# Decoding float64 weights in two VectorE passes instead of three, with an earlier weight schedule and fewer float32 products

## The chip, the core and the metric

The kernel runs on one core of a Trainium2 chip. A core has a matrix engine (TensorE, "PE" in the profile; its weight loads are listed apart as "PEld"), a vector engine (VectorE, "DVE"), an activation engine (ScalarE, "ACT"), a general engine (GpSimd, "POOL") and an engine that here only issues DMAs (SyncE, "SP"). Each engine works through its own list of instructions in the order in which they stand; engines wait for each other by semaphores. The metric is the device time of one execution in microseconds (us), the median of several runs.

## What is computed

Gated causal attention over 8 batches of 8 heads, 576 tokens, 64 values per head, followed by a normalisation and a two-layer feed-forward block with a residual. Cut to what matters:

```python
scores = (q @ k.T) / 8 + cum[:, None] - cum[None, :]     # cum: running sum of log(clip(f))
scores = where(causal, -1e9, scores)
attn   = softmax(scores)
x      = (attn @ v) put back to (8, 576, 512)
xn     = (x - mean(x)) / sqrt(var(x) + 1e-6) * g_ln
out    = x + relu(xn @ w_ch1) @ w_ch2                    # 512 -> 2048 -> 512
```

The two weight matrices arrive as float64; everything else is float32, and the result is float32.

## The kernel before

**Slots.** The 64 heads (`n`) are handled one after the other. A head's 576 query rows are cut into five tiles; tile 0 (64 rows) goes together with tile 1, so a head takes four slots (`t` = 1 to 4) and the attention takes 256 slots (`u`), with three more to drain. In each slot the letters of a string in `ORDERS` say in which order the pieces of work are written out, and this is the order on every engine's list: `Q` products of q and k, `S` mask and row maximum (VectorE), `e` exponential (ScalarE), `B` reciprocal and scaling (VectorE, GpSimd), and for tiles two slots older `t` transposes (TensorE), `h` copies (ScalarE), `l` their low parts (VectorE), then `A` the product with v (TensorE), `F` and `a` its write-out. There are three strings: for slots 0 to 36, 37 to 69, and from 70 on. `P` prepares later heads, with their loads.

**Two forms of products.** A head with `n < NFULL` multiplies with v in float32 (`fac` in `av_unit`; 3 products for the first half of a head and 5 for the second). Every later head splits both factors into a high and a low part of type fp32r and sums products of the parts (`acc` in `av_unit`; 5 and 9 products). The split form needs more around it: `prep_v` splits v (VectorE, GpSimd), `transposed_lo` makes the low parts of the transposed probabilities (VectorE), and the result comes in two halves, which `finish` and `finish_add` put together (ScalarE, VectorE). `NPLAIN = 8` does the same for q and k; it is not touched.

**Weights.** `WPrep` turns the float64 weights into fp32r parts on the chip, in 32 pieces of 128x512 numbers, alternately of layer 1 and layer 2. A float64 is seen as two 32-bit words, high `hw` and low `lw`. `load` brings the words in (512 KB a piece, three buffers `wr`); `scaled` reads the high word as a float32 and multiplies it by 2^-112 on ScalarE, which corrects the exponent (five buffers `wy`); `decode` works on bits, in VectorE passes; for layer 1 `colsum` multiplies with a constant (TensorE, tile `pc`) and `centre` adds the result (four VectorE instructions); `high` and `low` split the piece (ScalarE, GpSimd), and `keep` writes the low part of layer 2 to DRAM, from where it is read as `w2s`. `tick` moves all this on by one piece. How often it runs is set by a line under the letter `W`:

```python
due = 1 + min(u, W_CHANGE) / W_SLOTS + max(0, u - W_CHANGE) * W_TICKS
while not wp.done() and wp.tick_no <= due:
    wp.tick()
```

so a piece is due each `W_SLOTS` slots up to slot 34 and each 1/0.95 slots behind it. The VectorE instructions of a piece are put into `queue` and written out a few at a time by the letters `w` (1), `g` (2) and `f` (3), between the softmax instructions.

**Feed-forward steps.** The second part works on 18 chunks of 256 tokens, each in 16 steps: `mm1` is 12 matmuls with 256 columns (tile `h`), `mm2` 6 matmuls with 512 (tiles `acc`). From slot 35 on a slot takes one step along (letters `M`, `r`, `m`, `N`), where `can` allows it: the step's two weight pieces must be ready, and the chunk's heads done. What is left of the 288 steps behind the last slot runs alone, in the tail.

Of the kernel before, what the change touches and what calls it, by code (L numbers as in the profile page):

```python
# [8 lines left out]
F32 = mybir.dt.float32  # L9
# [3 lines left out]
AF = mybir.ActivationFunctionType  # L13
ALU = mybir.AluOpType
# [10 lines left out]
NEG = -1.0e9  # L25
SCALE = 1.0 / 8.0
NPLAIN = 8
NFULL = 16
W2_LOW = 3
W2_WAIT = 2  # L30
ALL = 2 * NCHUNK * FT + W2_WAIT
# [1 line left out]
FIRST_MOE = 35  # L33
WARM = 36

W_SLOTS, W_CHANGE, W_TICKS = 2.4, 34, 0.95
W_RAW, W_FLOAT = 3, 5
W_BORROW = 2
W_SUMS = 2
# [19 lines left out]
def attn_moe(ctx: ExitStack, tc: tile.TileContext, qk, v, f, g, w1, w2, out):  # L59
    nc = tc.nc  # L60
# [14 lines left out]
    def m2(name, dt):  # L75
        return work.tile([P, 512], dt, tag="m2", bufs=11, name=name)
# [9 lines left out]
    for i in range(WARM):  # L86
# [4 lines left out]
        out=mask[:, S - P :], in_=mask[:, S - P :], pattern=[[-1, P]], base=0,  # L91
# [42 lines left out]
    class WPrep:  # L134
# [21 lines left out]
        def scaled(self, n):  # L156
            layer, j = self.items[n]
            d = self.d[n]
            if layer == 1 and self.tick_no < W_BORROW:
                d["y"] = m2(f"wy{layer}_{j}", U32)  # L160
            else:
                d["y"] = wpool.tile([P, DM], U32, tag="wy", bufs=W_FLOAT, name=f"wy{layer}_{j}")
            nc.scalar.activation(d["y"].bitcast(F32), d["hw"].bitcast(F32), AF.Copy, scale=2.0**-112)

        def decode(self, n):
            layer, j = self.items[n]
            d = self.d[n]
            y, z, low = d["y"], d["hw"], d["lw"]
            d["w"] = y.bitcast(F32)
            ve = nc.vector  # L170

            return [
                lambda: ve.tensor_scalar(out=z, in0=z, scalar1=0x80000000, scalar2=None, op0=ALU.bitwise_and),
                lambda: ve.scalar_tensor_tensor(  # L174
                    out=y, in0=y, scalar=3, in1=z, op0=ALU.logical_shift_left, op1=ALU.bitwise_or
                ),
                lambda: ve.scalar_tensor_tensor(
                    out=y, in0=low, scalar=29, in1=y, op0=ALU.logical_shift_right, op1=ALU.bitwise_or
                ),
            ]  # L180

# [123 lines left out]
    def load(n):  # L305
        h = Head()
        h.n, h.plain, h.full = n, n < NPLAIN, n < NFULL
        if h.plain:
# [356 lines left out]
    class Moe:  # L665
# [21 lines left out]
        low = []  # L687
# [211 lines left out]
```

## Time and profile before

| | |
|---|---|
| median of 3 runs | 1253.7 us (1252.57, 1253.70, 1260.37) |
| profiled execution, first to last instruction | 1260.6 us |
| PE busy | 1230.2 us, 98% of the span |
| DVE busy | 782.8 us, 62% |
| ACT busy | 645.2 us, 51% |
| POOL busy | 426.8 us, 34% |
| DMA | 190.77 MB, mean 151 GB/s |
| chain that ended last | PE 86%, DVE 5%, DMA 4% |

The profile lists only the span of the profiled execution. It is as long as the slowest of the three timed runs, so there is next to nothing around it. A busy PE in this profile is not a PE at its peak, since the ends of matmuls are modelled; idle time of the PE is what its row lacks to the length of a stretch.

### The profile page before, as it was taken

The page shows a single profiled execution, that of the slowest core. Times are in us where ns is not written, and L with a number is a line of the kernel's source. Part 1 is how long each engine was busy: PE and PEld are TensorE (multiplying, and loading weights), DVE is VectorE, ACT ScalarE, POOL GpSimd, SP SyncE. Part 2 cuts the span into 40 slices and gives each one's busy share as a digit, 9 for nine tenths or more (in the row PEclk, how much of TensorE's full clock was granted, in tenths as well). Part 3 has the DMA queues.
Part 4 walks back from the last instruction along what each step waited for, and adds up shares of the span by engine and source line. Part 5 has one row for each costly group of instructions (what it writes and reads, how often), then busy time and mean ns, then how long its engine had stood idle before and what let it go on. Part 6 is the DMA issues. An engine that isn't in the chain of part 4 may idle for free.

```text
span 1260.6 us, 25515 instructions
## 1 busy us (share of the span) xinstructions
PE 1230.2 (98%) x8148; PEld 1085.2 (86%) x8148; DVE 782.8 (62%) x2868; ACT 645.2 (51%) x1920; POOL 426.8 (34%) x529
## 2 busy tenths in 40 slices
PE   8997898999999999999999999999999999999998
PEld 5554686889999999999999999999999999999997
DVE  5587888357576768576767666666767673233232
ACT  5577666555555556565656555655555552112111
POOL 3356556333343334334443434343434330000000
PEclk7799899999999999999999999999999999999999
DMA  5366674544554545444545454545454534444432
GB/s 154 110 183 204 198 240 160 159 124 155 154 165 148 168 141 171 137 150 149 156 144 160 145 168 151 168 151 166 149 152 147 168 104 136 125 126 117 151 109 92
DMA packets 139381, 190.77 MB, mean 151 GB/s; under 512 B 32496, under 2 KB 81648, under 8 KB 139248
## 3 DMA queue, kind: packets, MB, share of 16 engines
q1 hardware_dynamic: 139248, 189.15, 49.0%
q8 instruction: 65, 1.06, 0.3%
q14 instruction: 68, 0.56, 0.1%
HBM read 157.46 MB, written 23.36 MB: 143 GB/s over the span
## 4 chain that ended last, share of the span: by engine, by line
PE 86%; DVE 5%; DMA 4%; ACT 1%; POOL 1%; issue 1%; SPq 0%; DVEq 0%; POOLq 0%; ACTq 0%
PE h L580 11%; PE h L581 10%; PE h L582 10%; PE acc L602 10%; PE acc L603 10%; PE acc L604 10%; PE tr L418 7%; PE o L503 5%; PE o L481 3%; PE s L370 3%; PE s L371 3%; DMA raw<-in_qk_dram 3%; PE s L368 1%; PE xp L418 1%; DVE wy L174 1%
## 5 line engine op out<-in xcount | busy, mean ns | idle before, releaser
L412 POOL TENSOR_SCALAR p<-p,st 64x64 f32<-64x64 f32 (+4 forms) x320 | 173.8, 546 | 568.1 <-DVE st L411 225.9
L580 PE MATMUL h<-x,w1h 128*128 128x256 f32 x1152 | 329.6, 286 | 0.0
L581 PE MATMUL h<-x,w1h 128*128 128x256 f32 x1152 | 325.9, 283 | 0.7 <-DVE x L565 0.7
L582 PE MATMUL h<-x,w1l 128*128 128x256 f32 x1152 | 324.9, 282 | 0.0
L588 ACT ACTIVATE hh<-h 128x256 fp32r<-128x256 f32 x288 | 110.4, 383 | 287.7 <-PE h L582 281.0
L593 DVE SCALAR_TENSOR_TENSOR hh<-h,hh 128x256 fp32r<-128x256 f32 x288 | 121.4, 422 | 193.3 <-ACT hh L588 189.0
L602 PE MATMUL acc<-w2h,hh 128*128 128x512 f32 x576 | 228.1, 396 | 0.0
L603 PE MATMUL acc<-w2s,hh 128*128 128x512 f32 x576 | 226.4, 393 | 0.0
L604 PE MATMUL acc<-w2h,hh 128*128 128x512 f32 x576 | 225.7, 392 | 0.0
L580 PEld LDWEIGHTS h<-x,w1h 128*128 128x128 f32 x1152 | 218.2, 189 | 5.2 <-issue 0.9
L581 PEld LDWEIGHTS h<-x,w1h 128*128 128x128 f32 x1152 | 218.2, 189 | 4.6 <-DVE x L565 1.3
L582 PEld LDWEIGHTS h<-x,w1l 128*128 128x128 f32 x1152 | 218.0, 189 | 0.0
L405 ACT ACTIVATE p<-p,st 64x64 f32<-64x64 f32 (+4 forms) x320 | 178.3, 558 | 60.8 <-DVE st L394 58.1
L468 ACT CAST ph<-tr 64x128 fp32r<-64x128 f32 (+4 forms) x384 | 108.6, 332 | 110.4 <-PE tr L418 82.6
L418 PE MATMUL tr<-identr,p 128*128 128x128 f32 (+1 forms) x896 | 143.7, 277 | 9.0 <-POOL p L412 4.7
L394 DVE CUSTOM_DVE_ANT_0 p<-s,mask 64x64 f32<-64x64 f32 (+4 forms) x320 | 130.3, 420 | 15.5 <-PE s L368 9.8
L418 PEld LDWEIGHTS tr<-identr,p 128*128 128x128 f32 (+1 forms) x896 | 102.9, 132 | 35.3 <-POOL p L412 9.1
L604 PEld LDWEIGHTS acc<-w2h,hh 128*128 128x128 f32 x576 | 108.2, 188 | 25.3
L473 DVE TENSOR_TENSOR ph<-tr,ph 64x192 fp32r<-64x192 f32 x192 | 57.8, 301 | 106.1 <-ACT ph L468 102.9
L602 PEld LDWEIGHTS acc<-w2h,hh 128*128 128x128 f32 x576 | 108.7, 189 | 13.4 <-issue 0.9
L603 PEld LDWEIGHTS acc<-w2s,hh 128*128 128x128 f32 x576 | 109.0, 189 | 12.3
L370 PE MATMUL s<-hi 128*64 128x64 f32 x336 | 109.8, 349 | 8.3 <-POOL hi L348 6.5
(81 smaller groups left out, 1848.4 us busy)
## 6 DMA issues: line engine op xcount, KB each, us to landing
w2s<-w2d SPq DMA_DIRECT2D x288, 256.0 KB
raw<-in_qk_dram SPq DMA_DIRECT2D x56, 576.0 KB
wr<-in_w_dram SPq DMA_DIRECT2D x32, 512.0 KB
vr<-in_v_dram SPq DMA_DIRECT2D x64, 160.0 KB
out_dram<-xt SPq DMA_DIRECT2D x36, 256.0 KB
xq<-hi SPq DMA_DIRECT2D x56, 144.0 KB
xa<-xs SPq DMA_DIRECT2D x32, 160.0 KB
w2d<-wl SPq DMA_DIRECT2D x16, 256.0 KB
```

What stands on the lines that cost most here:

```text
L370: mm(sp, h.hi[:, 0, q0 : q0 + m], h.hi[:, 1, a:z], start=True, stop=False)
L394: nc.vector.tensor_tensor_reduce(out=pt[:m, a:z], in0=sp, in1=mask[:m, off + a : off + z], scale=-SCALE, scalar=3.0e38 if i == 0 else st[: ...
L405: nc.scalar.activation(pt[:m, :w], pt[:m, :w], AF.Exp, bias=st[:m, i : i + 1], scale=-1.0, accum_out=st[:m, 2:3])
L412: nc.gpsimd.tensor_scalar(out=pt[:m, :w], in0=pt[:m, :w], scalar1=st[:m, 3:4], scalar2=1.0, op0=ALU.mult, op1=ALU.mult)
L418: nc.tensor.transpose(out_, in_, ident[:m, :m])
L580: mm(ph, w1h[:, k, fs], c.x[k][:, 0, :], start=(k == 0), stop=False)
L581: mm(ph, w1h[:, k, fs], c.x[k][:, 1, :], start=False, stop=False)
L582: mm(ph, w1l[:, k, fs], c.x[k][:, 0, :], start=False, stop=(k == KT - 1))
L593: nc.vector.scalar_tensor_tensor(out=h[:, 1, :], in0=ph, scalar=0.0, in1=h[:, 0, :].bitcast(F32), op0=ALU.max, op1=ALU.subtract)
L602: mm(c.acc[i], h[:, 0, ts_], w2h[:, j, :], start=(j == 0), stop=False)
L603: mm(c.acc[i], h[:, 0, ts_], low, start=False, stop=False)
L604: mm(c.acc[i], h[:, 1, ts_], w2h[:, j, :], start=False, stop=(j == FT - 1))
```

## The change

`NFULL` goes from 16 to 12: heads 12 to 15 take the split form of the product with v. `W_SLOTS` goes from 2.4 to 1.6: up to slot 34 a weight piece is due each 1.6 slots. `scaled` uses a Relu with a slope for negative numbers in place of a scaled copy: positive numbers are multiplied by 2^-112, negative ones by 2^-112 times 2^32. The extra 32 in the exponent field of a negative number becomes its sign bit when the word is shifted left by 3, so the pass that kept the sign falls away: `decode` has a shift of the low word and one shift-and-or, no longer three passes.

```diff
-NFULL = 16
+NFULL = 12
...
-W_SLOTS, W_CHANGE, W_TICKS = 2.4, 34, 0.95
+W_SLOTS, W_CHANGE, W_TICKS = 1.6, 34, 0.95
...
-            nc.scalar.activation(d["y"].bitcast(F32), d["hw"].bitcast(F32), AF.Copy, scale=2.0**-112)
+            nc.scalar.activation(d["y"].bitcast(F32), d["hw"].bitcast(F32), AF.Prelu, scale=2.0**-112, alpha=2.0**32)
...
-                lambda: ve.tensor_scalar(out=z, in0=z, scalar1=0x80000000, scalar2=None, op0=ALU.bitwise_and),
+                lambda: ve.tensor_scalar(out=low, in0=low, scalar1=29, scalar2=None, op0=ALU.logical_shift_right),
                 lambda: ve.scalar_tensor_tensor(
-                    out=y, in0=y, scalar=3, in1=z, op0=ALU.logical_shift_left, op1=ALU.bitwise_or
-                ),
-                lambda: ve.scalar_tensor_tensor(
-                    out=y, in0=low, scalar=29, in1=y, op0=ALU.logical_shift_right, op1=ALU.bitwise_or
+                    out=y, in0=y, scalar=3, in1=low, op0=ALU.logical_shift_left, op1=ALU.bitwise_or
                 ),
```

Three lines fall away, so everything behind `decode` stands three lines higher in the changed kernel (L580 becomes L577).

What this does to the lists of the engines is seen in three places. The first is VectorE in slots 12 and 13 (head 3, tiles 1 and 2). `L394`/`L391` is mask and maximum, `L410`/`L407` and `L411`/`L408` are sum and reciprocal, `L173`, `L174` and `L177` are the passes of `decode`, `L194` is `centre`. Before:

```order
L394 ISA p_1_543,st_1_544<-s_1_0_534,mask 128x192
L394 ISA st_1_544 128x1
L174 SCALAR_TENSOR_TENSOR wy_3_505<-wy_3_505,wr_3_400 128x512
L177 SCALAR_TENSOR_TENSOR wy_3_505<-wr_3_400,wy_3_505 128x512
L410 TENSOR_SCALAR st_0_541<-st_0_541 64x1
L411 RECIPROCAL st_0_541<-st_0_541 64x1
L410 TENSOR_SCALAR st_1_544<-st_1_544 128x1
L411 RECIPROCAL st_1_544<-st_1_544 128x1
L394 ISA p_2_578,st_2_579<-s_2_0_576,mask 128x320
```

And in the changed kernel:

```order
L391 ISA p_1_564,st_1_565<-s_1_0_555,mask 128x192
L391 ISA st_1_565 128x1
L174 SCALAR_TENSOR_TENSOR wy_4_527<-wy_4_527,wr_4_423 128x512
L407 TENSOR_SCALAR st_0_562<-st_0_562 64x1
L408 RECIPROCAL st_0_562<-st_0_562 64x1
L407 TENSOR_SCALAR st_1_565<-st_1_565 128x1
L408 RECIPROCAL st_1_565<-st_1_565 128x1
L173 TENSOR_SCALAR wr_4_490<-wr_4_490 128x512
L391 ISA p_2_607,st_2_608<-s_2_0_605,mask 128x320
L391 ISA st_2_608 128x1
L194 SCALAR_TENSOR_TENSOR wy_3_420<-wy_3_420,gcol,pc_557 128x128
L174 SCALAR_TENSOR_TENSOR wy_4_582<-wy_4_582,wr_4_490 128x512
```

One large pass instead of two stands between maximum and reciprocal; but the next piece follows at once, and slot 13, which had no weight work, now has a large pass and the first part of a centring.

The second place is VectorE in slot 46 (head 11, tile 3), where `L593`/`L590` is a feed-forward step's `mm1_low` and `L565`/`L562` is `chunk_split`. Before:

```order
L394 ISA p_3_1929,st_3_1930<-s_3_0_1926,mask 128x448
L394 ISA st_3_1930 128x1
L174 SCALAR_TENSOR_TENSOR wy_13_1910<-wy_13_1910,wr_13_1784 128x512
L177 SCALAR_TENSOR_TENSOR wy_13_1910<-wr_13_1784,wy_13_1910 128x512
L593 SCALAR_TENSOR_TENSOR hh_8_1978<-h_8_1948,hh_8_1978 128x256
L410 TENSOR_SCALAR st_3_1930<-st_3_1930 128x1
L411 RECIPROCAL st_3_1930<-st_3_1930 128x1
L565 TENSOR_TENSOR x_0_1991<-xr_0_1916,x_0_1991 128x256
L173 TENSOR_SCALAR wr_13_1859<-wr_13_1859 128x512
```

In the changed kernel:

```order
L391 ISA p_3_1987,st_3_1988<-s_3_0_1984,mask 128x448
L391 ISA st_3_1988 128x1
L194 SCALAR_TENSOR_TENSOR wy_15_1785<-wy_15_1785,gcol,pc_1931 128x128 x3
L590 SCALAR_TENSOR_TENSOR hh_8_2031<-h_8_2001,hh_8_2031 128x256
L407 TENSOR_SCALAR st_3_1988<-st_3_1988 128x1
L408 RECIPROCAL st_3_1988<-st_3_1988 128x1
L562 TENSOR_TENSOR x_0_2043<-xr_0_1974,x_0_2043 128x256
```

The last weight piece is centred here, and no weight work stands on VectorE from slot 47 on; before, it went on to slot 53.

The third place is TensorE in slot 52 (head 13, tile 1; the product with v is that of head 12). `L481` is the float32 product, `L500` the split one, `L189` is `colsum`, `L602` and `L603` belong to `mm2`, `L577` to `L579` are `mm1`. Before:

```order
L189 MATMUL pc_2307<-wy_15_2171,gneg 128x128 x4
L418 MATMUL tr_3_2313<-identr,p_3_2202 64x128
L418 MATMUL tr_3_2313<-identr,p_3_2202 128x128 x3
L481 MATMUL o_2_2318<-ph_12_2210,vr_1965 64x320
L481 MATMUL o_2_2318<-ph_12_2210,vr_1965 64x256
L481 MATMUL o_2_2318<-ph_12_2210,vr_1965 64x128
L602 MATMUL acc_0_1498<-w2h,hh_11_2284 128x512
L603 MATMUL acc_0_1498<-w2s_2243,hh_11_2284 128x512
```

In the changed kernel:

```order
L415 MATMUL tr_3_2370<-identr,p_3_2237 64x128
L415 MATMUL tr_3_2370<-identr,p_3_2237 128x128 x3
L500 MATMUL o_2_2375<-ph_12_2240,vv_2269 128x320
L500 MATMUL o_2_2375<-ph_12_2240,vv_2269 128x256
L500 MATMUL o_2_2375<-ph_12_2240,vv_2269 128x128
L500 MATMUL o_2_2375<-pl_12_2241,vv_2269 64x256
L500 MATMUL o_2_2375<-pl_12_2241,vv_2269 64x128
L577 MATMUL h_14_2381<-x_0_1436,w1h 128x256
L578 MATMUL h_14_2381<-x_0_1436,w1h 128x256
L579 MATMUL h_14_2381<-x_0_1436,w1l 128x256
```

Before, slots 48, 50, 52, 54 and 56 have no `mm1`, because the weights aren't there yet; in the changed kernel each of them has one, and slot 70 lacks one instead (its chunk's heads aren't there). Both lists start with `mm1` in slot 38. Behind slot 255 there are 76 steps left before and 72 now.

More of the change, by code (lines that the diff above doesn't have):

```diff
@@ L167, in decode @@
             d = self.d[n]
-            y, z, low = d["y"], d["hw"], d["lw"]
+            y, low = d["y"], d["lw"]
             d["w"] = y.bitcast(F32)
```

## The prediction

> **What bounds the kernel now.** I read the stages first, since the whole-span shares mix stages with different limits. In this view, busy time by stretch, the columns are length, busy us and instructions (x) of each engine, granted TensorE clock, DMA share and GB/s.
>
> ```profile
> core 0: us, PE busy (x) PEld busy (x) DVE busy (x) ACT busy (x) POOL busy (x), PEclk, DMA share, GB/s
> 11.00:52.00 41.00, 39.31 (x133) 24.34 (x131) 22.84 (x86) 20.74 (x65) 11.80 (x18) 0.63 0.47 130
> 52.00:96.00 44.00, 40.77 (x198) 24.82 (x196) 33.67 (x124) 31.34 (x99) 22.07 (x27) 0.96 0.55 161
> 96.00:137.00 41.00, 28.12 (x138) 18.25 (x138) 30.30 (x91) 26.55 (x79) 26.95 (x28) 0.88 0.62 191
> 137.00:185.00 48.00, 48.00 (x317) 40.70 (x316) 43.98 (x116) 30.93 (x84) 27.19 (x26) 1.00 0.72 227
> 185.00:225.00 40.00, 35.71 (x221) 27.89 (x220) 29.90 (x102) 26.68 (x79) 23.11 (x25) 1.00 0.52 169
> 400.00:900.00 500.00, 499.76 (x3532) 460.34 (x3532) 347.95 (x1359) 289.68 (x877) 193.19 (x245) 1.00 0.51 156
> 1040.00:1240.00 200.00, 200.00 (x1297) 182.20 (x1297) 58.04 (x173) 37.72 (x99) 0.00 (x0) 1.00 0.43 128
> ```
>
> From 225 us on TensorE never waits, so there only its own work counts. Before that it idles 12.9 us in 96 to 137 and 4.3 us in 185 to 225. In 137 to 185 TensorE is full and VectorE nearly so (92%). In 11 to 52 TensorE is full at 0.63 of its clock. The stretches are, by slot: 0 to 27 up to 96 us, 28 to 37 up to 137, 38 to 47 up to 185, 48 to 57 up to 225.
>
> The same view for the tile `h` alone counts feed-forward steps: 12 matmuls, one VectorE and one ScalarE instruction each.
>
> ```profile
> core 0: us, PE busy (x) PEld busy (x) DVE busy (x) ACT busy (x), PEclk, DMA share, GB/s
> 185.00:225.00 40.00, 8.39 (x60) 7.48 (x60) 2.09 (x5) 1.83 (x5) 1.00 0.52 169
> 400.00:900.00 500.00, 196.44 (x1467) 187.39 (x1466) 51.75 (x123) 47.31 (x123) 1.00 0.51 156
> 1040.00:1240.00 200.00, 110.98 (x832) 107.63 (x831) 29.61 (x70) 26.88 (x70) 1.00 0.43 128
> ```
>
> In the tail a step takes 200/70 = 2.86 us of TensorE. A slot with a step takes 500/123 = 4.07 us, so the attention part of a slot with split products is 1.21 us. In 185 to 225 there are only 5 steps in ten slots: the weights come too late for more.
>
> **The change part by part.** The chain that ended last, in order of time, shows a head's product with v in both forms, on a TensorE that waits for nothing:
>
> ```profile
> 252.69 1.47 PE o L481 x6
> 261.57 2.23 PE o L481 x10
> 271.28 0.50 PE o L503 x5
> 278.74 0.94 PE o L503 x9
> ```
>
> *Four heads in split form.* In float32 the two halves of a head take 1.47 + 2.23 = 3.70 us, in split form 0.50 + 0.94 = 1.44. Heads 12 to 15 do this from slot 51 to 66, where TensorE sets the time: 4 x 2.26 = **-9.0 us**. What the split form adds lies on other engines. By form:
>
> ```profile
> L473 DVE TENSOR_TENSOR pl<-tr,ph 128x384 fp32r<-128x384 f32 x96 | 53.6, 558 | 2.2
> L473 DVE TENSOR_TENSOR ph<-tr,ph 64x128 fp32r<-64x128 f32 x144 | 40.9, 284 | 65.9 <-ACT ph L468 63.7 <-ACT ot L537 0.3
> L354 DVE CAST vv<-vr 128x320 fp32r<-128x320 f32 x48 | 23.1, 481 | 1.8 <-PE o L481 1.8
> L548 DVE TENSOR_TENSOR xs<-o,ot 64x320 f32<-64x320 f32 x48 | 23.1, 481 | 0.7
> ```
>
> These and their smaller forms come to some 4.7 us of VectorE a head, 1.2 a slot. The stretch 400 to 900 already holds them and has VectorE at 348 of 500 us, 2.8 of each slot's 4.07; so TensorE hides them, provided that no weight work is left there. None is: VectorE's list ends it in slot 46. If 2.2 us of weight work a slot still lay there, VectorE would need 5.0 us and the gain would be gone.
>
> *Steps that come earlier.* Slots 48, 50, 52, 54 and 56 get their step, and TensorE has the time for it: its idle 4.3 us in 185 to 225. Where it loses them is seen in the timeline:
>
> ```profile
> 188.32 0.67 ACT L337 CAST hi<-raw 128x576 fp32r<-128x576 f32 x1 [2.56 <-DMA raw<-in_qk_dram]
> 192.75 0.47 PE L370 MATMUL s<-hi 128*128 128x448 f32 x1 [1.83 <-DVE st L394]
> ```
>
> VectorE with its weight queue (and a head's load, which stays) is late, and TensorE has no step to fill the gap. With a step in every slot it has. I take **-4.3 us**, all of it; the ends are 0 and -6 (a busy TensorE is not quite a full one, since the ends of matmuls are modelled). The five steps come out of the tail; slot 70 lacks one, which costs nothing if TensorE stays fed in it, and at most a step, 2.9 us: **+1**.
>
> *`colsum` moves ahead.* Its rows by stretch:
>
> ```profile
> 11.00:52.00 41.00, 4.99 (x24) 4.86 (x24) 0.63 0.47 130
> 185.00:225.00 40.00, 2.13 (x16) 2.02 (x16) 1.00 0.52 169
> ```
>
> The 16 records in the full stretch go (-2.1 us). One piece more, 8 records at 0.21 us, falls into 11 to 52, where TensorE is full too (+1.7): **-0.4** together.
>
> *Two passes.* These are the groups of weight work:
>
> ```profile
> L174 DVE SCALAR_TENSOR_TENSOR wy<-wy,wr 128x512 uint32<-128x512 uint32 x32 | 35.3, 1103 | 0.0
> L177 DVE SCALAR_TENSOR_TENSOR wy<-wr,wy 128x512 uint32<-128x512 uint32 x32 | 30.2, 945 | 0.6
> L173 DVE TENSOR_SCALAR wr<-wr 128x512 uint32<-128x512 uint32 x32 | 16.9, 528 | 0.8 <-ACT wy L163 0.8
> L197 DVE SCALAR_TENSOR_TENSOR wy<-wy,gcol,pc 128x128 f32<-128x128 f32 x64 | 20.7, 337 | 0.0
> L163 ACT ACTIVATE wy<-wr 128x512 f32<-128x512 f32 x32 | 21.5, 671 | 8.3 <-POOL w1l L218 3.6 <-DMA wr<-in_w_dram 2.7 <-POOL wl L218 1.9
> L214 ACT CAST w1h<-wy 128x512 fp32r<-128x512 f32 x16 | 9.9, 617 | 17.3 <-DVE wy L197 17.2
> L218 POOL TENSOR_TENSOR w1l<-wy,w1h 128x512 fp32r<-128x512 f32 x16 | 22.7, 1416 | 0.1
> ```
>
> A piece costs VectorE 0.53 + 1.10 + 0.94 + 0.67 (half of four times 0.337) = 3.25 us now, and 2.30 without L177. The shift takes L173's place with the same tile, so I take 0.53 for it (at best nothing, at worst L174's 1.10). The Relu with a slope isn't in the trace; I take the scaled copy's 0.67 us, the nearest row; the ends are L214's 0.62 for as many elements and two full passes, 1.34.
>
> For the SBUF page of the Trainium skill (SBUF — State Buffer, section "SBUF: two separate sides") a VectorE instruction with two inputs and a GpSimd one exclude each other for a whole instruction. The trace agrees: the medians by tile are 1.06 us for L174 and 0.69 for L177, with equal minima. By that rule the wait falls on whichever two-input pass comes first behind GpSimd, and the dropped one is the cheap one: a piece gets 0.69 us cheaper, not 0.94. That would take 1 us off the next term.
>
> *96 to 137 us.* From slot 34 on a piece is due each 1.05 slots in both kernels, so VectorE gets 0.9 us a slot lighter. What stood there:
>
> ```profile
> 107.48 4.56 DMA raw<-in_qk_dram
> 121.38 4.93 DMA raw<-in_qk_dram
> ...
> 131.91 0.82 PE L418 MATMUL tr<-identr,p 128*64 128x128 f32 x3 [4.12 <-DVE wy L197]
> 132.66 4.20 PE L481 MATMUL o<-ph,vr 64*64 64x256 f32 x10
> ```
>
> The two loads of `raw` are in the chain and stay: there is one such buffer, and the next load waits for the last reader. The 4.12 us of idle TensorE are a PSUM bank that late `centre` work holds, and the product behind it takes 4.20 us instead of 2.23, at half the clock. Four slots at 0.9 us are 3.8 of VectorE's; I take **-4 us**. The bounds are 0 (the loads set the pace anyway) and -9 (the stall, the slow product and some more of the 12.9 idle us).
>
> *Slots 0 to 33.* Pieces each 1.6 slots mean 0.21 more of them a slot: VectorE 0.625 x 2.30 = 1.44 us instead of 0.417 x 3.25 = 1.36, ScalarE +0.27 (L163 and L214), GpSimd +0.29 (L218). No engine is near its limit by that (in 52 to 96 VectorE has 34 of 44 us, ScalarE 31, GpSimd 22), but softmax instructions queue behind this work on each. The order helps: between maximum and reciprocal, where VectorE waits for the exponential anyway, L174 alone stands now instead of L174 and L177. I take **+1 us**; the ends are -3 (0.1 us a slot better) and +9 (all of ScalarE's 0.27 us in 34 slots). The piece loads have room: L163 waited 2.7 us for them in all, and DMA is at 0.55.
>
> 137 to 185 stays at its floor, TensorE. The sum is -9.0 - 4.3 + 1 - 0.4 - 4 + 1 = -15.7 us on the profiled execution's 1260.6, which is as long as the slowest run (1260.37), 6.9 above the median. I carry the same difference to the median: 1253.7 - 15.7 = **1238 us**.
>
> **The rivals.**
>
> *Early slots pay.* The chain in 96 to 137 runs through the `raw` loads, so a lighter VectorE brings nothing there, and ScalarE's added work delays every exponential: -9.0 - 4.3 + 1 - 0.4 + 0 + 9 = -3.7, **1250 us**. For it speaks that the loads are in the chain; against it that the late `centre` stalled TensorE for 4 us.
>
> *Everything early loosens.* The stall and both slow products in 96 to 137 go (-9), slots 0 to 33 gain 3 us, and slot 70 costs nothing: -9.0 - 4.3 - 0.4 - 9 - 3 = -25.7, **1228 us**.
>
> *The clock stays low: slower than before.* Exponentials counted by stretch, with the granted clock in the column behind them:
>
> ```profile
> 14.00:44.00 30.00, 6.33 (x20) 0.50 0.41 108
> 61.40:96.00 34.60, 10.37 (x32) 1.00 0.63 185
> ```
>
> A head has ten such records, so a slot took 3.75 us at half the clock and 2.70 at full. It came back at 44 us; more ScalarE and GpSimd work ahead of the transposes could open gaps on TensorE that keep it low up to slot 37: 26 slots x 1.05 = +27, the gain in 96 to 137 is lost, and -9.0 - 4.3 + 1 - 0.4 + 1 + 27 = +15.3 gives **1269 us**. From some 11 such slots on (11.7 / 1.05) the kernel is slower than before. Against it: in 52 to 96 the clock was 0.96 though TensorE had gaps. The Trainium skill (TensorE: Matmul & The Clock Gate, Part 1) says that a window of some 3.4 us without enough activity halves the clock; the row above agrees with the two rates, and the 4.12 us gap at 128 is the kind that it means.
>
> *It doesn't do what it says.* VectorE, not TensorE, sets slots 48 to 66, because weight work hangs over from slot 46: the -9.0 and -4.3 shrink to some -6 together (less than half), and 1253.7 - 6 + 1 - 0.4 - 4 + 1 = **1245 us**.
>
> **How the numbers follow.** Forecast (1231 to 1244) 0.53, everything loosens 0.17, early slots pay 0.18, hang-over 0.07, low clock 0.05. A measurement tells 1% from no change, here 1241.2 and 1266.2. Faster by over 1% are the looser case and nearly all of the forecast, 0.68; within 1% the early and the hang-over case and the forecast's upper end, 0.27; slower the low clock, 0.05. The range reaches from below the looser case (a Relu or shift at their good ends adds little) to the early case's end: 1222 to 1251.
>
> **What would show it.** A step in each slot from 38 to 69 and no idle TensorE in 185 to 225; L500 at 0.50 and 0.94 us in heads 12 to 15; 72 steps behind the last slot; L163 at 0.67 us and L173 at 0.53; slot 28 reached near 96 us and slot 48 near 182; no 4 us stall behind `centre`. Wrong would make it: a slower L163, slots 0 to 33 longer by more than 3 us, half the clock behind 60 us, or VectorE over 4 us a slot in slots 48 to 51.

## The result and the profile after

The changed kernel takes **1240.1 us** (median of 4 runs, 1238.05 to 1240.83), the kernel before 1253.1 us beside it (4 runs, 1250.88 to 1260.37): a ratio of 0.9869, 95% interval [0.983, 0.9909]. That is 13.0 us less; 1238 had been forecast, from 15.7 us less. The ratios given here and below are not the quotients of the two medians; that would be 0.9896 here.

The two profiled executions differ by more, 21.6 us:

```profile
span 1239.0 us, 25554 instructions
...
PE 1215.1 (98%) x8140; PEld 1080.7 (87%) x8140; DVE 767.6 (62%) x2884; ACT 647.6 (52%) x1920; POOL 427.3 (34%) x533
...
PEclk8997999999999999999999999999999999999999
...
PE 89%; DVE 3%; ACT 2%; DMA 2%; POOL 1%; issue 1%; SPq 0%; DVEq 0%; POOLq 0%; ACTq 0%
```

The profiled execution of before was one of its long ones (1260.6 us of span), that of after an ordinary one (1239.0 us of span in a run of 1240.83, 0.7 us over the median). So the stretches of before and after must not be subtracted without asking which difference another execution would show again. The busy time by stretch of the changed kernel:

```profile
core 0: us, PE busy (x) PEld busy (x) DVE busy (x) ACT busy (x) POOL busy (x), PEclk, DMA share, GB/s
11.00:52.00 41.00, 36.67 (x168) 22.44 (x166) 29.81 (x114) 28.92 (x88) 17.97 (x26) 0.88 0.72 204
96.00:137.00 41.00, 35.69 (x182) 25.60 (x181) 29.39 (x94) 27.99 (x78) 27.48 (x27) 0.83 0.71 220
137.00:185.00 48.00, 48.00 (x305) 39.78 (x304) 24.32 (x88) 28.97 (x85) 26.68 (x27) 1.00 0.56 172
185.00:225.00 40.00, 40.00 (x280) 36.56 (x279) 28.41 (x111) 21.03 (x64) 14.50 (x19) 1.00 0.45 142
217.00:282.00 65.00, 60.81 (x417) 55.29 (x416) 41.96 (x164) 32.79 (x100) 23.81 (x29) 0.97 0.47 146
400.00:900.00 500.00, 499.75 (x3531) 460.36 (x3531) 347.86 (x1348) 288.05 (x874) 195.93 (x246) 1.00 0.50 155
```

Three things are to be seen. TensorE has no idle time left in 185 to 225, where it had 4.3 us (these are slots 50 to 59 here and 48 to 57 before; slots 48 to 57, 173.64 to 217.44 us here, are full as well, 43.80 of 43.80 us). VectorE has 24.32 us of work in 137 to 185 in place of 43.98, and TensorE stays full there. And there is a new hole: in 217 to 282 TensorE lacks 4.2 us, at a clock of 0.97, where the prediction let it wait for nothing.

The same view for the tile `h` alone shows ten feed-forward steps in 185 to 225 in place of five (slots 48 to 57 hold ten too):

```profile
185.00:225.00 40.00, 16.65 (x120) 14.92 (x120) 4.22 (x10) 3.75 (x10) 1.00 0.45 142
```

The weight work by groups (line, engine, operation, busy us and mean ns, idle time before with what ended it):

```profile
L163 ACT ACTIVATE wy<-wr 128x512 f32<-128x512 f32 x32 | 21.4, 670 | 10.8 <-POOL wl L215 5.1 <-DMA wr<-in_w_dram 3.2 <-POOL w1l L215 2.4
L173 DVE TENSOR_SCALAR wr<-wr 128x512 uint32<-128x512 uint32 x32 | 17.4, 544 | 0.0
L174 DVE SCALAR_TENSOR_TENSOR wy<-wy,wr 128x512 uint32<-128x512 uint32 x32 | 34.9, 1091 | 0.1
L211 ACT CAST w1h<-wy 128x512 fp32r<-128x512 f32 x16 | 9.8, 615 | 3.3 <-DVE wy L194 3.3
L415 PE MATMUL tr<-identr,p 128*64 128x128 f32 x320 | 77.4, 273 | 5.5 <-ACT xs L531 2.3 <-POOL p L409 2.2 <-DVE st L391 0.9
```

The Relu with a slope costs what the scaled copy cost, 0.670 us, and the shift 0.544. ScalarE's `high` waits 3.3 us for `centre` in all, where it waited 17.2, and in the row of the transposes, the last, a PSUM bank held by `centre` ends no wait any more.

**The new wait** stands at the start of slot 64. SyncE's own queue first, then ScalarE, VectorE, TensorE and GpSimd in the timeline (start, length, instruction; in brackets the idle time ahead of it and what ended it):

```profile
237.00 0.43 SPq L610 DMA_DIRECT2D xw<-xa  x1
...
240.33 1.33 SPq L610 DMA_DIRECT2D xw<-xb  x1
241.76 0.38 SPq L692 DMA_DIRECT2D w2s<-w2d  x1
242.18 0.44 SPq L316 DMA_DIRECT2D raw<-in_qk_dram  x1
```

```profile
246.53 0.67 ACT L334 CAST hi<-raw 128x576 fp32r<-128x576 f32 x1 [3.84 <-DMA raw<-in_qk_dram]
...
248.87 0.42 DVE L590 SCALAR_TENSOR_TENSOR hh<-h,hh 128x256 fp32r<-128x256 f32 x1 [5.29 <-ACT hh L585]
...
249.34 0.38 PE L577 MATMUL h<-x,w1h 128*128 128x256 f32 x1 [2.73 <-DVE st L407]
...
249.70 0.71 POOL L409 TENSOR_SCALAR p<-p,st 64x64 f32<-64x64 f32 x2 [7.81 <-DVE st L407]
```

Eight small loads (`rows_load` of chunk 1, whose steps now come five earlier) occupy SyncE's queue from 237.00 to 241.66, and the load of a head's `raw` is issued behind them. ScalarE stands at `hi<-raw` for 3.84 us; behind it in its list are the exponentials and the feed-forward's Relu, so VectorE, GpSimd and in the end TensorE stand too. The chain that ended last goes this way: the load of `raw` takes 4.26 us from its issue, then ScalarE, VectorE and TensorE follow. Before, chunk 1 ran five steps later, and its loads did not stand ahead of this `raw`.

### The profile page after: what moved, and what is told of

It is laid out like the page before. It is cut to its first block, busy times and chain, and to the rows that moved or that the text cites. A ratio compares the mean times of both kernels' runs of the same rounds, so it can differ in the third digit from the quotient of the medians.

```text
span 1239.0 us, 25554 instructions
## 1 busy us (share of the span) xinstructions
PE 1215.1 (98%) x8140; PEld 1080.7 (87%) x8140; DVE 767.6 (62%) x2884; ACT 647.6 (52%) x1920; POOL 427.3 (34%) x533
## 4 chain that ended last, share of the span: by engine, by line
PE 89%; DVE 3%; ACT 2%; DMA 2%; POOL 1%; issue 1%; SPq 0%; DVEq 0%; POOLq 0%; ACTq 0%
PE h L577 11%; PE h L578 11%; PE h L579 11%; PE acc L599 11%; PE acc L600 10%; PE acc L601 10%; PE tr L415 7%; PE o L500 6%; PE s L367 3%; PE s L368 3%; PE o L478 2%; PE xp L415 1%; DMA raw<-in_qk_dram 1%; PE s L365 1%; PE pc L186 1%
## 5 line engine op out<-in xcount | busy, mean ns | idle before, releaser
L577 PE MATMUL h<-x,w1h 128*128 128x256 f32 x1152 | 330.1, 287 | 3.5 <-DVE st L407 2.7
L579 PE MATMUL h<-x,w1l 128*128 128x256 f32 x1152 | 325.2, 282 | 0.0
L590 DVE SCALAR_TENSOR_TENSOR hh<-h,hh 128x256 fp32r<-128x256 f32 x288 | 121.5, 422 | 187.0 <-ACT hh L585 174.2
L577 PEld LDWEIGHTS h<-x,w1h 128*128 128x128 f32 x1152 | 218.4, 190 | 8.5 <-DVE st L407 3.0
L579 PEld LDWEIGHTS h<-x,w1l 128*128 128x128 f32 x1152 | 218.3, 189 | 0.0
L465 ACT CAST ph<-tr 64x128 fp32r<-64x128 f32 (+4 forms) x416 | 117.9, 332 | 131.1 <-PE tr L415 100.8
L415 PE MATMUL tr<-identr,p 128*128 128x128 f32 (+1 forms) x896 | 141.2, 274 | 5.5 <-ACT xs L531 2.3
L391 DVE CUSTOM_DVE_ANT_0 p<-s,mask 64x64 f32<-64x64 f32 (+4 forms) x320 | 130.2, 419 | 7.7 <-PE s L368 2.8
L470 DVE TENSOR_TENSOR ph<-tr,ph 64x192 fp32r<-64x192 f32 x208 | 62.6, 301 | 114.5 <-ACT ph L465 111.6
```

What stands on the lines that cost most here:

```text
L391: nc.vector.tensor_tensor_reduce(out=pt[:m, a:z], in0=sp, in1=mask[:m, off + a : off + z], scale=-SCALE, scalar=3.0e38 if i == 0 else st[: ...
L415: nc.tensor.transpose(out_, in_, ident[:m, :m])
L577: mm(ph, w1h[:, k, fs], c.x[k][:, 0, :], start=(k == 0), stop=False)
L579: mm(ph, w1l[:, k, fs], c.x[k][:, 0, :], start=False, stop=(k == KT - 1))
L590: nc.vector.scalar_tensor_tensor(out=h[:, 1, :], in0=ph, scalar=0.0, in1=h[:, 0, :].bitcast(F32), op0=ALU.max, op1=ALU.subtract)
```

## The experiments

Each kernel ran beside runs of the kernel before on its chip; the ratio is to these. They took 1255.8 us (median of 27) beside the first four experiments and 1256.9 us (median of 11) beside the four from the changed kernel again to ten float32 heads. Because executions of one kernel differ early and agree late, I read every profile in two parts: up to the start of slot 48 (VectorE's first mask instruction of that slot), and from there to the end. In all of these kernels ten steps lie ahead of slot 48.

```
                                  slot 28   slot 34   slot 48      end    slot 48 to end
before                               95.9     115.1     184.9   1260.6        1075.8
heads alone                          84.0     105.5     175.0   1247.4        1072.3
two passes alone                     86.2     108.5     175.8   1248.3        1072.4
two passes and early slots           88.8     107.9     171.4   1242.5        1071.0
heads and early slots, three passes 101.6     121.5     189.1   1253.5        1064.4
changed                              88.2     108.2     173.6   1239.0        1065.4
changed, again                       89.0     108.2     175.6   1241.0        1065.4
rows loaded earlier                  90.6     110.0     175.4   1234.9        1059.5
  and a piece each 1.4 slots         92.8     114.7     180.1   1239.8        1059.7
  and ten float32 heads              92.6     115.1     179.4   1240.6        1061.2
```

The last column repeats to 0.1 us in the two profiles of the changed kernel, and in five profiles of the kernel in the last line it was 1059.2 to 1061.6. The first columns can move much further: see the second experiment.

### The parts one by one

**Two passes alone.** Against the changed kernel:

```diff
-NFULL = 12
+NFULL = 16
-W_SLOTS, W_CHANGE, W_TICKS = 1.6, 34, 0.95
+W_SLOTS, W_CHANGE, W_TICKS = 2.4, 34, 0.95
```

> The kernel before with the two-pass decoding alone (a piece each 2.4 slots, 16 float32 heads). Theory A (the TensorE account of the prediction: the gain is the four heads and the steps that come earlier, and slots 0 to 33 gain nothing): the weights still come too late for steps in slots 48 to 57, only stalls behind a late VectorE go, some 2 us in 96 to 137 and some 2 in 185 to 225, so 1249 us, ratio 0.997. Theory B (the two passes shorten the early softmax chain and keep TensorE's clock up, as the profile after suggests, where slot 28 is reached 7.6 us earlier): most of that stays, 1244 us or less, ratio 0.992 or less.

Measured: 1250.1 us (10 runs), ratio 0.9952 [0.9927, 0.9976], so theory A's size. From slot 48 on the kernel is 3.4 us shorter (1075.8 to 1072.4) though it still misses the five steps. TensorE's idle time in slots 48 to 57 (175.85 to 213.60 us here) goes all the same, with VectorE lighter there (33.24 us of work in 50, where the kernel before has 29.90 in 40):

```profile
175.00:225.00 50.00, 49.22 (x310) 38.95 (x309) 33.24 (x121) 32.92 (x98) 27.98 (x30) 1.00 0.62 197
```

**Heads alone.** Against the kernel before:

```diff
-NFULL = 16
+NFULL = 12
```

> The kernel before with float32 products in 12 heads, three passes and a piece each 2.4 slots. Theory A: weight work stays on VectorE up to slot 53, beside the split heads' 1.2 us a slot, so slots 48 to 53 are bound by VectorE at 5 us or more and a good part of the 9.0 us is lost: 1249 us, ratio 0.996. Rival (TensorE sets these slots anyway): the full 9 us, 1244 us, ratio 0.993.

Measured: 1250.4 us (12 runs), ratio 0.9963 [0.9936, 0.9989]. Of the 9.0 us for four heads only 3.5 show from slot 48 on. VectorE still has weight work there and now splits heads as well: it has 41.92 us of work in 50, and TensorE lacks 7.9 us. Of the waits that the profile lists for TensorE in 174 to 226, 7.3 us end on VectorE and 0.4 on GpSimd:

```profile
175.00:225.00 50.00, 42.08 (x267) 35.16 (x266) 41.92 (x143) 29.91 (x88) 28.97 (x31) 0.97 0.49 157
```

This is the hang-over rival's mechanism, seen where the schedule was not moved. The same profile tells something else. VectorE's list is that of the kernel before, in the same order, up to slot 48, and yet it reaches slot 28 at 84.0 us and not at 95.9, and slot 48 at 175.0 and not at 184.9:

```profile
11.00:52.00 41.00, 36.82 (x175) 22.78 (x175) 30.30 (x115) 27.87 (x89) 17.62 (x26) 0.92 0.58 159
```

The clock granted in 11 to 52 was 0.92 here and 0.63 in the profile of before. So the earlier marks of the changed kernel (slot 28 at 88.2) are no gain by themselves.

**Two passes and early slots,** without the heads. Against the changed kernel:

```diff
-NFULL = 12
+NFULL = 16
```

> The changed kernel with 16 float32 heads again. Theory A: the heads 12 to 15 cost TensorE 9.0 us more than in the changed kernel, and nothing hides them: 1249 us, ratio 0.996 to before. Rival (the split heads' extra VectorE and ScalarE work takes their gain back, so the heads bring nothing): 1240 us, ratio 0.990.

Measured: 1244.2 us (6 runs), ratio 0.9914 [0.9891, 0.9938], between the two theories and nearer to the rival; theory A's 0.996 lies outside the interval. From slot 48 on it is 4.8 us shorter than before, and the changed kernel is 5.6 us shorter still, so the heads do bring something and the rival's reason is wrong. What brings this kernel so low lies ahead of slot 48 (see the account of the prediction). The same eight loads stand ahead of `raw` here, but ScalarE waits 1.79 us, and TensorE, with float32 products still to do, hardly lacks anything:

```profile
218.00:285.00 67.00, 66.56 (x430) 56.08 (x429) 32.97 (x140) 32.55 (x100) 22.22 (x28) 1.00 0.44 137
```

**Heads and early slots with three passes.** Against the kernel before:

```diff
-NFULL = 16
+NFULL = 12
-W_SLOTS, W_CHANGE, W_TICKS = 2.4, 34, 0.95
+W_SLOTS, W_CHANGE, W_TICKS = 1.6, 34, 0.95
```

> The changed kernel with the three-pass decoding again: a piece each 1.6 slots and 12 float32 heads stay. Theory A: a piece costs VectorE 3.25 us, 2.0 a slot up to slot 33 instead of 1.4, and between maximum and reciprocal two large passes stand again; slots 0 to 33 get 0.2 to 0.5 us longer each, and slots 34 to 44 are full on VectorE: 1250 to 1258 us, ratio 0.998 to 1.004. Rival (the earlier schedule and the heads do it alone, the dropped pass was hidden): 1240 us, ratio 0.990.

Measured: 1250.9 us (12 runs), ratio 0.9962 [0.9945, 0.9979], close to theory A. This is the kernel that shows what the passes are for. From slot 48 on it is as fast as the changed kernel (1064.4 and 1065.4), so heads and schedule bring the whole of the late gain without them. But it is slower in all: 4.9 us under the kernel before beside it, where the changed kernel is 13.0 and 15.3 us under it in its two sets of runs. That lies ahead of slot 48, which its profile reaches at 189.1 us and the changed kernel's at 173.6. The profiled run was its longest, 4.4 us over its median; some 11 us are left. VectorE's share grows in the early stretch:

```profile
11.00:52.00 41.00, 36.65 (x159) 22.43 (x157) 32.91 (x115) 27.63 (x83) 18.93 (x26) 0.83 0.70 190
```

With three passes, a piece each 1.6 slots costs early what it brings late; the ratio is the one of heads alone.

### The new wait

**The changed kernel again,** as the base of the next three on one chip.

> The changed kernel itself, timed beside the next three on the same chip: 1240 us, ratio 0.987.

Measured: 1241.6 us (6 runs), ratio 0.9863 [0.9826, 0.9899]; ScalarE's wait for `raw` at slot 64 was 4.04 us this time.

**Rows loaded earlier.** The first half of chunk 1's rows is loaded one step earlier, so that the eight loads no longer stand just ahead of `raw`:

```diff
-                if c.j in (FT - 7, FT - 5):
-                    rows_load(c, (c.j - (FT - 7)) // 2)
+                first = FT - 8 if c.n == 1 else FT - 7
+                if c.j in (first, FT - 5):
+                    rows_load(c, 0 if c.j == first else 1)
```

> The changed kernel with the first row loads of chunk 1 issued one step earlier, so that eight small loads no longer stand ahead of a raw load on SP's queue at slot 63. Theory A (what the four heads lost was this new wait: ScalarE waits 3.84 us for raw at slot 64, TensorE 2.73 us, and then runs 3.4 us at half the clock): 3 to 4 us less than the changed kernel, 1236 to 1237 us, ratio 0.984, and no idle TensorE near slot 64. Rival (the raw load waits for its buffer anyway and takes its 4 to 5 us, whatever is ahead of it): within 1 us of the changed kernel, ratio 0.987.

Measured: **1235.8 us** (6 runs, 1234.68 to 1236.83), ratio 0.9817 [0.9778, 0.9856]: 5.8 us below the changed kernel beside it, whose fastest run took 1238.47. Counted from the start of slot 48, the load of `raw` is issued 64.4 us on, where it was 68.5 in the first profile of the changed kernel. ScalarE's wait is 0.24 us, and the stretch is full:

```profile
244.68 0.68 ACT L334 CAST hi<-raw 128x576 fp32r<-128x576 f32 x1 [0.24 <-DMA xw<-xb]
```

```profile
241.00:256.00 15.00, 15.00 (x108) 13.71 (x106) 9.27 (x35) 8.74 (x26) 6.03 (x8) 1.00 0.44 148
217.00:282.00 65.00, 63.90 (x447) 58.30 (x447) 44.90 (x174) 35.94 (x111) 25.39 (x31) 1.00 0.50 157
```

In the changed kernel the stretch 241 to 256 had 12.27 us of TensorE at a clock of 0.89. The late part falls from 1065.4 to 1059.5, 5.9 us, so all of the gain lies from slot 48 on. It is more than the 2.7 us of idle time and more than the 3 to 4 us of theory A. The hole also cost clock: the trace of the changed kernel has half the clock for some 3.4 us, 249.9 to 253.3, so 1.7 us of work at full clock. These two make 4.4 us, near the 4.6 by which slots 48 to 67 get shorter (91.2 to 86.6). The other 1.3 us come behind slot 67, in a part that takes 972.9 to 974.7 us in the kernels with early slots; their cause is not shown. This is the fastest version that ran.

**A piece each 1.4 early slots,** on top of that:

```diff
-W_SLOTS, W_CHANGE, W_TICKS = 1.6, 34, 0.95
+W_SLOTS, W_CHANGE, W_TICKS = 1.4, 34, 0.95
```

> The last kernel with a piece each 1.4 slots in slots 0 to 33. Theory A: 0.09 pieces more a slot bring VectorE 0.2 us a slot there, and slots 0 to 33 aren't bound by it: within 2 us of the last kernel, 1235 to 1239 us. Rival (early slots pay for each piece, some 2 us of in-order work each): three more pieces by slot 34, 4 to 6 us slower, 1241 us or more.

Measured: 1242.0 us (6 runs), ratio 0.9868 [0.9832, 0.9904], 6.2 us slower. The late part is the same (1059.7), slot 34 comes at 114.7 us in place of 110.0. From here on, more pieces in the early slots are paid for there.

**Ten float32 heads,** on top of both:

```diff
-NFULL = 12
+NFULL = 10
```

> The last kernel with float32 products in 10 heads, not 12: heads 10 and 11 go to the split form, in slots 40 to 50. Theory A: weight work ends in slot 43 here, so three slots have both and VectorE costs them up to 1 us each; TensorE gains 2 x 2.26 us: 2 to 4 us less than the last kernel, 1232 to 1235 us, ratio 0.981. Rival (VectorE, not TensorE, sets slots 38 to 47): no gain or a loss, 1237 us or more.

Measured: 1240.8 us (6 runs), ratio 0.9868 [0.9828, 0.9908]: 1.2 us less than with twelve, a miss for the 2 to 4 us of theory A. Heads 10 and 11 are multiplied in slots 43 to 50, and TensorE no longer sets the time there; it lacks 1.9 us in a stretch that was full with twelve (47.84 of 48):

```profile
137.00:185.00 48.00, 46.11 (x310) 40.31 (x311) 29.31 (x112) 28.44 (x85) 22.59 (x25) 1.00 0.49 147
```

The profile shows what it waits for: `raw` again. In slot 48 ScalarE stands 2.23 us for the load of a head, and TensorE 1.30 us behind it; in slot 56 it is 3.82 and 1.27 us. With twelve float32 heads ScalarE stood 0.74 and 1.14 us at these two places and TensorE not at all. Ten heads and then, in the last line, twelve:

```profile
181.79 0.67 ACT L334 CAST hi<-raw 128x576 fp32r<-128x576 f32 x1 [2.23 <-DMA raw<-in_qk_dram]
...
184.61 0.39 PE L577 MATMUL h<-x,w1h 128*128 128x256 f32 x1 [1.30 <-DVE st L407]
```

```profile
182.21 0.67 ACT L334 CAST hi<-raw 128x576 fp32r<-128x576 f32 x1 [0.74 <-DMA raw<-in_qk_dram]
```

All five profiles of the kernel with ten heads have both holes on TensorE, of 1.16 to 2.25 and of 0.98 to 1.38 us. So the rival came true in its time, but by a late load and not by VectorE's work. What holds these loads up was not tested.

**Four more runs** were meant for 16 and for 10 float32 heads and for a piece each 1.9 slots on the kernel with the rows loaded earlier, and for that kernel once more. By a mistake in the file all four ran the kernel of the experiment just told, ten heads and 1.4 slots, so their expectations, which speak of kernels that did not run, decide nothing, and no run answers these three questions. What they give is how well a median repeats: on a chip of their own, 6 runs each, 1240.2, 1241.2, 1239.7 and 1240.6 us, ratios 0.9856 to 0.9873. Differences of under some 1.5 us between kernels of one chip, such as the 1.2 us above, are not told apart by six runs; the 5.8 and 6.2 us are.

## Why the prediction was right, and where it was not

The total came out 2.7 us short of the forecast difference, because a loss that was not foreseen, 5.9 us by the wait at slot 64, was made up in part by gains larger than forecast. That it came out so near is partly luck. By its steps:

- **Four heads, -9.0.** Two pairs differ in the heads. In the changed kernel the late part falls from 1071.0 to 1065.4 us, 5.6; with the new wait out of the way, to 1059.5, 11.5. Counted over slots 48 to 67 alone it is 96.3 us without the split heads, 91.2 changed, 86.6 with the rows loaded earlier: 5.1 and 9.7. The first and the last of these three are full on TensorE at full clock. First two passes and early slots with 16 float32 heads, then the kernel with the rows loaded earlier:

```profile
171.45:218.90 47.45, 47.45 (x298) 38.85 (x297) 20.20 (x90) 24.15 (x74) 15.50 (x20) 1.00 0.46 149
218.90:267.75 48.85, 48.85 (x311) 40.23 (x310) 18.10 (x79) 22.71 (x70) 13.99 (x18) 1.00 0.43 133
```

```profile
175.39:219.33 43.94, 43.94 (x297) 38.58 (x297) 27.25 (x112) 24.43 (x74) 16.72 (x21) 1.00 0.46 150
219.33:261.98 42.65, 42.65 (x308) 39.54 (x307) 27.44 (x105) 23.00 (x69) 16.13 (x20) 1.00 0.47 150
```

So the moved loads had no idle time to give back to the kernel with 16 float32 heads there, as far as a busy TensorE can tell, and the 9.7 us are the heads: the term had its size, and the wait at slot 64 took about half of it. (The kernel with the rows moved and 16 float32 heads did not run, and the 1.8 us by which the two differ behind slot 67 have no cause shown.)

The step that failed is the sentence "From 225 us on TensorE never waits, so there only its own work counts". That held for the kernel before (65.00 of 65 us in 225 to 290), with float32 products in slots 51 to 66 and a chunk 1 that came later; taking 9 us of work out of it and moving the chunk's loads put a transfer on the path that had been hidden. Neither alone did: with the loads moved and 16 float32 heads TensorE is full, as shown, and with the split heads alone it is full in slots 58 to 67 (38.5 of 38.5 us in 219 to 257.5). The prediction counted a moved step's matmuls, and forgot the loads that it issues and the queue on SyncE in which they stand.

- **Steps that come earlier, -4.3, slot 70 +1, `colsum` -2.1 late.** Together -5.4; the kernel with two passes and early slots, without heads, is 4.8 shorter from slot 48 on. The idle 4.3 us are gone as forecast. But 3.4 of the 4.8 come with the lighter VectorE alone, so what filled TensorE was mostly that it no longer waited for VectorE, and less that it had a step to do meanwhile.
- **96 to 137 us, -4; slots 0 to 33, +1; one more piece of `colsum`, +1.7.** Together -1.3 ahead of slot 48. The marks that were forecast, slot 28 near 96 us and slot 48 near 182, were passed at 88.2 and 173.6, but one profile of a start that moves by 10 us decides nothing. So take the medians, less the 2.1 and 1.8 us that a run takes over its span, and less the late parts: slot 48 comes at 1253.1 - 2.1 - 1075.8 = 175.2 us before and 1240.1 - 1.8 - 1065.4 = 172.9 after, -2.3. The later runs of the changed kernel, with the kernel before beside them, give 179.0 and 174.4 us, -4.6, and two passes and early slots without the heads 177.9 and 171.4, -6.5. So the sign is right and the forecast rather too small; how much is gained early is known to some us only, and the terms are not shown one by one. What is shown is the cause: without the two passes the same schedule costs some 10 to 12 us more early (it reaches slot 48 at 184.7 us by the same working), and a still earlier one costs 6.2. The rival that early slots pay was wrong for 1.6 and right for 1.4 slots.
- **Two passes.** A piece costs VectorE 0.544 + 1.091 + 0.67 = 2.31 us (2.30 forecast). The whole mean of the dropped pass went, 0.94 us. The Trainium skill (SBUF — State Buffer, section "SBUF: two separate sides") states that a VectorE instruction with two SBUF inputs and a GpSimd instruction that reads SBUF shut each other out for a whole instruction. From this the prediction considered that the remaining pass would take over the dropped one's waits, and save only 0.69. The trace doesn't bear that out: L174 takes 1.091 us on average after 1.103.
- **The clock.** It did not stay low (0.88 in 11 to 52, where before had 0.63, and 0.83 in 96 to 137, where before had 0.88), so the slower rival fell.
- **The carry from profile to median.** 15.7 us were subtracted from the median although the profile of before was a long execution. It was longer than it was taken for: runs of this kernel take some 2.1 us more than their span, so a span of 1260.6 us belongs to a run of some 1262.7, 9 us above the median and not 6.9, and slower than all three timed runs. The late terms repeat within some 2 us, so the carry was sound for them; the term for 96 to 137 us was read from a stall of that one execution, and there it was luck.

Late, -10.4 us were measured where -14.4 had been forecast; without the wait it is -16.3. Early, it is -2.3 where -1.3 had been forecast. (These add up to the -13.0 measured, but for 0.3 us around the spans, because the early part was worked out as what the late one leaves; the sum confirms nothing.)

## What to carry to other kernels

When a step moves, list the transfers that it issues and what stands behind them in that queue: eight small loads, 4.7 us on SyncE's queue, were enough to make a full TensorE wait. Time taken from the engine that sets the pace uncovers what it had hidden, so look for the next late transfer in the very stretch that gets shorter; with ten float32 heads it was `raw` once more, in slots 48 and 56. And before two profiles are subtracted, read them from a mark behind the unsteady start: the late part repeated within 2.4 us, the early one moved by 10 us under the same instructions.

## What was not expected of the hardware

A hole of 2.73 us on TensorE was followed by some 3.4 us at half its clock; these are 7 us of the changed kernel around slot 64, and the half-clock part of them:

```profile
247.00:254.00 7.00, 4.66 (x20) 4.19 (x20) 4.20 (x16) 4.43 (x15) 2.57 (x4) 0.76 0.28 83
249.60:253.10 3.50, 3.50 (x16) 3.21 (x16) 3.32 (x11) 1.88 (x6) 2.09 (x3) 0.54 0.25 63
```

In the fourteen profiles, behind 140 us, each hole of 2.25 us or more (2.25, 2.73, 2.93 and 3.05) was followed by such a stretch. Of the five holes of 1.8 to 2.0 us one was (1.85), the others were not (1.82, 1.83, 1.83, 2.00), and none of the shorter ones was.

And the time of one kernel moves with the clock that it is granted: 27 runs of the kernel before on one chip lay between 1251.7 and 1267.5 us, and the six of them whose mean clock was 0.983 or less took 1257.2 to 1267.5. The changed kernel's runs lay within 2.8 us in one set and 5.2 in another.
